# One new order for a whole backward pass: parameter gradients released early, and the dense branch put into the row order of the inverse transforms

## The chip, the cores and the metric

The kernel runs on one core of one Trainium2 chip. The core has five engines that work side by side: TensorE (PE in the profile, with its weight loads apart as PEld), VectorE (DVE), ScalarE (ACT), GpSimd (POOL) and SyncE (SP). Data moves between the chip's memory and the core's working memory by DMAs, which SP, ACT and POOL issue. The metric is the device time of one execution in microseconds (us). Before the change three executions took 793.69, 794.1 and 794.8 us, a median of 794.1.

## The reference

The forward pass mixes two branches with a gate that is worked out from each row of the input. The kernel returns the output and the gradients of fourteen of the inputs (15 results).

```python
def _A_ref(u, A_re, A_im, B_re, B_im, C_re, C_im, log_dt, Dskip):   # D = 448 channels, N = 256 states
    P = jnp.exp(logdA[:, :, None] * l[None, None, :])                # l = 0 .. 2047, rounded to bf16
    K = jnp.einsum("dn,dnl,dn->dl", Cc, P, dB).real
    ...                                                              # rfft of K and u, padded to 4096
    y = irfft(Uf * Kf)[:, :, 0, :L]
    y = y.transpose(0, 2, 1) + u * Dskip
    return y
def _B_ref(x, w1, b1, w2, b2):                                       # F = 1792
    h = relu(x @ w1 + b1) ** 2
    return h @ w2 + b2
g = sigmoid((x * gate_w).sum(-1, keepdims=True))                     # x is A_u, 2048 rows of 448
out = g * _A_ref(x, ...) + (1 - g) * _B_ref(x, ...)
# returned: out and the vjp of grad_out for A_u, the six A/B/C arrays, log_dt, Dskip, w1, b1, w2, b2, gate_w
```

## The kernel before, in words

The kernel is written in two steps. `build` records tasks: each is one instruction, one DMA, or a group of matmuls into one bank, with the tasks that it depends on. Two long lists in the file then fix everything. `ORDER` says in which order the tasks are emitted, and so the order of each engine's instructions; an entry is four times the task's number, plus a number that picks one of the engines or queues which the task allows (a copy can be ACT's or DVE's, a DMA SP's or POOL's). `HOMES` gives each buffer its place in one arena of working memory or in one of eight banks. An engine takes its instructions strictly in its part of the list, and SP and POOL take their DMAs so too. `R.dep` adds a dependency on a task that shares no data, so that a load does not start before a chosen moment.

All engine work is emitted from the helper's lines, which is why the profile knows only few lines: L1585 is every matmul, L1587 every transpose on PE, L1593 every activation, L1595 copies and DMAs, L1597 the other vector instructions, L1589 the transposing DMAs. Tiles of the arena all have the name "arena". Groups are told apart by their shapes.

The stages, in the order in which they begin:

- Forward transforms of the input `U` and of the gated gradient `DA` (`fwd1`, `fwd2`), their products, and a first inverse for the gradient of the convolution kernel K (lines 825 to 873). The spectra are stored to `sp_d`.
- Dense branch, forward (lines 1030 to 1051), in eight blocks of 256 rows. `turned` (line 1014) transposes a block on PE with the identity `ident` as the moving operand. `project` (line 975) writes the branch's result rows to a scratch tensor `br_d`.
- The gradient of w2 (lines 1053 to 1068): `DB2`, the whole of grad_out, is loaded in one DMA into a place that the dense branch has just left, and scaled by 1 - g on ACT and DVE (`omg32`). Then the dense branch's backward blocks (lines 1083 to 1105), which write a second `br_d` part and `dh_d`.
- Beside these, seven chunks c = 0 .. 6 of the state space. `tables(c)` (line 1159) builds powers X and Y and multiplies them into K's sums on PE; `gT[c]` is the last step of X. `gradient(c, h)` (line 1226) forms, for each half h, two products on DVE of 128x5376 and sums on PE, and stores 256 sums per row to `st_d`; `gG` holds its ends. `gG[11]` is chunk 5 done, `gG[13]` chunk 6.
- The gradient of w1 (lines 1270 to 1296): `U2`, the whole input, in one DMA; `dh_d` comes back through transposing DMAs on SP.
- The convolution kernel itself (lines 1298 to 1344): K's sums, `fwd1` and `fwd2` of K, eight products of 128x3584 with the stored spectra (`product`, two DVE instructions each; `gQ[0]` .. `gQ[7]`), and for each `inv1`, the first inverse stage, which stores to `hd[1]` (for the output) or `hd[2]` (for the gradient of the input). Each is read back whole, in another layout, by `load_hs`.
- The two last stages. Output (lines 1376 to 1394): for q = 0 .. 3 `load_hs`, `load_br`, the second inverse stage on PE, and per bank two instructions of DVE with 128x448 results (lines 1388 and 1389), 32 in all; their row sums give the gate's gradient. Gradient of the input (lines 1397 to 1415): the same loads from the other scratch tensors, PE, a copy, and the store. The rows of this stage lie in the order of the inverse transforms: partition 32 g + i holds what in the natural order is partition 4 i + g. So `load_br` uses four DMAs of 32 partitions.
- The gradient of gate_w (line 1416 on): the gate's gradient `ds_b` is first put back into natural rows with a matmul by `perm`, then multiplied with `U2`.
- Parameter gradients (line 1433 on; PR below), in two halves: chunks 0 to 3, with 128x512 operands, and chunks 4 to 6, with 128x384. Each half loads the sums `ST`, `pg` and `raw`, does 35 to 36 DVE instructions and two on ACT. Eight groups of transposes on PE, a sum for log_dt, and 24 stores follow. The loads of the first half depend on `gQ[0]`, those of the second on `gQ[6]`.

In the old list DVE has 834 instructions. The first half of PR has its places from 698 to 748, the second from 741 to 787, the last product of the spectra is at 737, and the output stage's instructions lie from 776 to 830, mixed with PR's last. On PE (779 tasks) the first inverse stages for `hd[1]` lie from 683 to 751, those for `hd[2]` from 716 to 747; PR's transposes are at 752 to 761, the output stage at 754 to 769. On SP the load of `ST0` is number 111.

Of the kernel before, what the change touches and what calls it, by code (L numbers as in the profile page):

```python
# [16 lines left out]
P = 128  # L17
L, D, N, F = 2048, 448, 256, 1792
LT = L // P
# [428 lines left out]
def replay(R, order, homes):  # L448
# [169 lines left out]
def build(nc, R, A_u, Ap, A_log_dt, A_Dskip, B_w1, B_b1, B_w2, B_b2, gate_w, grad_out, outs):  # L618
# [100 lines left out]
    s32, g32, omg32, omg2 = (R.buf(n, 32) for n in ("s32", "g32", "omg32", "omg2"))  # L719
    s_b, omg_b, gg = (R.buf(n, w) for n, w in (("s_b", 16), ("omg_b", 16), ("gg", 32)))  # L720
    g_b, gp_b = Sub(gg, 0), Sub(gg, 16)
    gt32, gpt_b = R.buf("gt32", 32), R.buf("gpt_b", 16)
    junk = R.buf("junk", 448)
    R.rank = 2.0
    for t in range(LT):
        V("scalar_tensor_tensor", out=junk.v(0, [[1, D]]), in0=U.v(D * t, [[1, D]]), scalar=1.0, in1=gwb.v(0, [[1, D]]), op0=MUL, op1=MUL, accum_out=s32.f(t, [[1, 1]]))
    al = [[1, LT]]
# [900 lines left out]
```

## Time and profile before

| what | value |
|---|---|
| median of the runs | 794.1 us |
| the profiled execution's own time | 792.28 us |
| span of its instructions | 790.5 us |
| PE busy | 649.5 us (82%) |
| DVE busy | 570.6 us (72%) |
| ACT busy | 472.8 us (60%) |
| POOL busy | 154.5 us (20%) |
| granted TensorE clock, mean | 0.929 |
| moved by DMA | 138.06 MB, mean 175 GB/s |

The busy time of PE counts modelled ends of pipelined matmuls, so a busy PE can still be short of its peak. "DMA share" is the mean busy share of the core's 16 DMA engines. Times in windows and rows count from the first instruction.

### The profile page before, as it was taken

How to read it: one execution, taken by the hardware profiler on the slowest of the kernel's cores; microseconds unless marked ns; L12 is line 12 of the kernel's file. 1: busy time of each engine (PE TensorE's matmuls, PEld its weight loads, DVE VectorE, ACT ScalarE, POOL GpSimd, SP SyncE). 2: the span in 40 equal slices, each digit the busy share in tenths (PEclk: the TensorE clock that was granted, in tenths of full speed). 3: DMA queues.
4: the chain of work that ended last, by engine and by line, in shares of the span. 5: the costliest groups of instructions: out<-in, count | busy, mean ns of one | idle time of the engine just before them, and what ended most of it. 6: DMA issues, size and time to landing. Idle time of an engine off the chain costs nothing.

```text
span 790.5 us, 24859 instructions
## 1 busy us (share of the span) xinstructions
PE 649.5 (82%) x11046; PEld 437.3 (55%) x11046; DVE 570.6 (72%) x866; ACT 472.8 (60%) x708; POOL 154.5 (20%) x262
## 2 busy tenths in 40 slices
PE   4678898969999789688887998798398889975577
PEld 4665466547676456365665766584366454652212
DVE  4698788759758878965984889379624168999882
ACT  4999988569779666546753464164234386645214
POOL 5312232210101111100111021001001101545342
PEclk9878999989999899999999999999799999999558
DMA  9637889652414455736552352416833654899995
GB/s 278 215 137 252 312 286 315 225 147 106 127 74 153 165 139 126 145 72 97 165 140 93 107 177 71 150 36 206 166 71 133 163 121 161 271 316 293 311 291 174
DMA packets 120366, 138.06 MB, mean 175 GB/s; under 512 B 75666, under 2 KB 103108, under 8 KB 119620
## 3 DMA queue, kind: packets, MB, share of 16 engines
q1 hardware_dynamic: 98148, 61.16, 29.5%
q0 software_dynamic: 18816, 73.63, 27.8%
q10 hardware_dynamic: 3296, 1.70, 0.8%
q8 instruction: 86, 1.41, 0.7%
q14 instruction: 20, 0.16, 0.1%
HBM read 60.01 MB, written 60.16 MB: 152 GB/s over the span
## 4 chain that ended last, share of the span: by engine, by line
PE 52%; DVE 18%; DMA 11%; ACT 10%; issue 7%; POOL 1%; ACTq 0%; SPq 0%; DVEq 0%; POOLq 0%
PE banks L1585 52%; DVE arena L1597 16%; ACT arena L1595 7%; DMA arena<-in_grad_out_dram 4%; DMA arena<-hd 3%; DVE arena L1595 2%; ACT arena L1593 2%; DMA hd<-arena 2%; DMA arena<-in_A_u_dram 1%; DMA arena<-br_d 1%; DMA arena<-in_B_w_dram 1%; ACT L1593 0%; POOL hd L1595 0%; POOL arena L1595 0%; ACTq L1595 0%
## 5 line engine op out<-in xcount | busy, mean ns | idle before, releaser
L1585 PE MATMUL banks<-arena 128*32 128x42 bf16 (+10 forms) x10998 | 643.9, 250 | 123.6 <-DVE arena L1597 39.6
L1585 PEld LDWEIGHTS <-arena 128*32 128x32 bf16 (+5 forms) x10994 | 432.4, 103 | 331.3 <-issue 180.2
L1597 DVE TENSOR_TENSOR arena<-arena 128x256 bf16<-128x256 bf16 (+13 forms) x502 | 385.7, 814 | 47.5 <-ACT arena L1593 25.1
L1595 ACT CAST arena<-banks 128x896 bf16<-128x896 f32 (+4 forms) x411 | 313.9, 827 | 165.3 <-PE banks L1585 138.9
L1595 DVE CAST arena<-banks 128x1024 bf16<-128x1024 f32 (+5 forms) x73 | 74.9, 1040 | 86.6 <-PE banks L1585 73.7
L1593 ACT ACTIVATE arena<-arena 128x256 f32<-128x256 f32 (+7 forms) x136 | 76.2, 583 | 48.9 <-DVE arena L1597 28.3
L1595 POOL DMA_DIRECT2D out_dram<-arena x60 | 32.5, 544 | 178.4 <-ACT arena L1595 98.9
L1597 DVE TENSOR_TENSOR arena<-banks,arena 128x1024 bf16<-128x1024 f32 (+2 forms) x46 | 40.5, 891 | 30.3 <-PE banks L1585 16.6
L1595 ACT COPY arena<-banks 128x168 f32<-128x168 f32 (+3 forms) x35 | 14.6, 427 | 60.7 <-PE banks L1585 49.7
L1597 DVE SCALAR_TENSOR_TENSOR arena<-arena 128x128 f32<-128x128 f32 (+1 forms) x86 | 30.2, 351 | 16.3 <-DMA arena<-in_A_u_dram 10.5
L1595 ACT COPY arena<-arena 128x256 bf16<-128x256 bf16 (+4 forms) x59 | 30.1, 553 | 14.3 <-DVE arena L1597 11.1
L1593 ACT ACTIVATE arena<-banks 128x1024 bf16<-128x1024 f32 (+1 forms) x29 | 26.0, 909 | 7.3 <-PE banks L1585 6.9
L1595 POOL DMA_DIRECT2D hd<-arena x36 | 23.0, 642 | 35.3 <-ACT arena L1595 30.6
L1595 POOL DMA_DIRECT2D br_d<-arena x21 | 11.7, 556 | 90.3 <-ACT arena L1595 90.1
L1595 ACT CAST arena<-arena 128x768 bf16<-128x768 f32 (+3 forms) x28 | 21.8, 789 | 9.9 <-DVE arena L1597 9.9
L1597 DVE SCALAR_TENSOR_TENSOR arena<-banks,arena 128x448 bf16<-128x448 f32 x32 | 19.8, 649 | 5.7 <-PE banks L1585 3.1
L1595 POOL DMA_DIRECT2D r_d<-arena x14 | 11.6, 825 | 61.7 <-ACT arena L1593 46.5
L1597 DVE TENSOR_SCALAR arena<-arena 128x448 bf16<-128x448 bf16 (+9 forms) x51 | 18.3, 394 | 6.9 <-PE banks L1585 5.1
L1595 POOL DMA_DIRECT2D dh_d<-arena x5 | 5.5, 1109 | 59.3 <-DVE arena L1597 44.4
L1587 PE MATMUL banks<-arena 128*128 128x128 bf16 (+1 forms) x48 | 5.8, 305 | 12.2 <-DVE arena L1597 12.2
L1595 POOL DMA_DIRECT2D st_d<-arena x8 | 4.4, 550 | 53.3 <-ACT arena L1595 53.3
L1595 POOL DMA_DIRECT2D arena<-in_grad_out_dram x19 | 11.7, 619 | 15.4 <-PE banks L1585 11.1
(46 smaller groups left out, 92.6 us busy)
## 6 DMA issues: line engine op xcount, KB each, us to landing
r_d<-arena POOLq DMA_DIRECT2D x14, 896.0 KB, 5.8
arena<-hd SPq DMA_DIRECT2D x12, 896.0 KB, 8.2
hd<-arena POOLq DMA_DIRECT2D x36, 224.0 KB, 6.4
sp<-arena POOLq DMA_DIRECT2D x7, 896.0 KB, 6.0
arena<-sp POOLq DMA_DIRECT2D x6, 896.0 KB, 8.7
dh_d<-arena POOLq DMA_DIRECT2D x5, 896.0 KB, 6.0
arena<-r_d SPq DMA_DIRECT2D x5, 896.0 KB, 6.1
out_dram<-arena POOLq DMA_DIRECT2D x28, 112.0 KB, 4.5
```

The lines of the kernel that those rows point to most:

```text
L1585: fn(out, **kw)
L1587: fn(out, kw["in_"], kw["ident"], **({"tile_position": kw["tile_position"]} if "tile_position" in kw else {}))
L1593: fn(out, kw.pop("in_"), kw.pop("func"), **kw)
L1595: fn(out, kw["in_"])
L1597: fn(out=out, **kw)
```

## The change

Five edits to the recording, and new lists for all of it:

1. PR's loads, both halves, depend on `gT[6]` (the last step of X for chunk 6) and, as before, on the sums that they read: the first half on chunks 0 to 3, the second on chunks 4 to 6 only for `ST1`.
2. The dense branch's rows take the order of the inverse transforms: `turned` multiplies by `perm` where it multiplied by `ident`, `DB2` and `U2` are loaded in four DMAs of 32 partitions each, and `DB2` is scaled by a turned `omgt32`, for which two small DVE instructions are added beside `gt32`.
3. `load_br` becomes one DMA of 128 partitions, eight times.
4. The matmul by `perm` and the copy ahead of the gradient of gate_w go away, with the second load of `perm`.
5. `ORDER` and `HOMES` are replaced as a whole: 2738 entries for 2757, 809 buffers for 810.

What the new list does around PR, read with the task numbers shifted by the added and removed tasks: DVE has 852 instructions. PR's first half lies from 669 to 717, among the last steps of chunk 6's tables (632 to 698) and ahead of the second product pair of chunk 5. Its second half lies from 757 to 796 (one scaling of `raw` earlier, at 674). The last product of the spectra is at 797 and 798, and the output stage follows from 799 to 848. On PE (778 tasks) chunk 6's gradient sums come at 641 and 666 (they were at 702 and 735), the first inverse stages for `hd[1]` from 681 to 723, those for `hd[2]` from 672 to 760, PR's transposes from 728 to 751, the sum for log_dt at 750, the output stage from 761 to 768. On SP the loads of `ST0`, `pg` and the second `pg` are numbers 83, 84 and 86, behind two quarters of `U2` and one transposing DMA, and ahead of seven more; on POOL both `raw` loads are numbers 162 and 163. Of the output stage's `load_hs`, one is ahead of the store of log_dt's row on SP (131) and three behind it (132, 133, 136). The last `load_hs` of the input's gradient has the place of the second half of `Gt`, which the output stage's last instructions read.

```diff
 ORDER = [
...
 HOMES = [
...
-    gt32, gpt_b = R.buf("gt32", 32), R.buf("gpt_b", 16)
+    gt32, gpt_b, omgt_b, omgt32 = R.buf("gt32", 32), R.buf("gpt_b", 16), R.buf("omgt_b", 16), R.buf("omgt32", 32)
...
+    V("tensor_scalar", out=omgt_b.v(0, al), in0=gt32.f(0, al), scalar1=-1.0, scalar2=1.0, op0=MUL, op1=ADD)
+    V("tensor_copy", out=omgt32.f(0, al), in_=omgt_b.v(0, al))
...
-        rh = ident.v(0, [[1, 128]])
+        rh = perm.v(0, [[1, 128]])
...
-    R.dma(DB2.v(0, [[1, LT * D]]), d(G2, 0, [[LT * D, P], [1, LT * D]]), ANY)
+    for g in range(4):
+        R.dma(DB2.v(0, [[1, LT * D]], 32 * g, 32), d(G2, g * LT * D, [[4 * LT * D, 32], [1, LT * D]]), ANY)
     for t in range(LT):
-        scaled(DB2.v(D * t, [[1, D]]), DB2.v(D * t, [[1, D]]), omg32.f(t, [[1, 1]]))
+        scaled(DB2.v(D * t, [[1, D]]), DB2.v(D * t, [[1, D]]), omgt32.f(t, [[1, 1]]))
...
-    R.dma(U2.v(0, [[450, 16], [1, D]]), d(u2, 0, [[LT * D, P], [D, 16], [1, D]]), ANY)
+    for g in range(4):
+        R.dma(U2.v(0, [[450, 16], [1, D]], 32 * g, 32), d(u2, g * LT * D, [[4 * LT * D, 32], [D, 16], [1, D]]), ANY)
...
-    perm = const("perm", q=("POOL",), rank=300.0)
...
-        for g in range(4):
-            R.dma(br.v(0, [[2 * D, 2], [1, 2 * D]], 32 * g, 32), d(br_d, w * P * LT * D + g * LT * D + 2 * q * D, [[4 * LT * D, 32], [8 * D, 2], [1, 2 * D]],
-                  [("br", w, 2 * q + x + 8 * hp) for x in range(2) for hp in range(2)]), ANY if g % 2 else ("POOL", "SP"))
+        R.dma(br.v(0, [[2 * D, 2], [1, 2 * D]]), d(br_d, w * P * LT * D + 2 * q * D, [[LT * D, P], [8 * D, 2], [1, 2 * D]], [("br", w, 2 * q + x + 8 * hp) for x in range(2) for hp in range(2)]), ANY)
...
-    ps = R.ps("dsn")
-    dsn = R.buf("dsn", 16)
-    R.group("PE")
-    mm(ps.f(0, al), perm.v(128, [[1, 128]]), ds_b.v(0, al), True, True)
-    R.end(also=[dsn])
-    V("tensor_copy", out=dsn.v(0, al), in_=ps.f(0, al))
...
-        mm(ps.f(0, [[1, D]], 0, 1), dsn.v(t, [[1, 1]]), U2.v(450 * t, [[1, D]]), t == 0, t == LT - 1)
+        mm(ps.f(0, [[1, D]], 0, 1), ds_b.v(t, [[1, 1]]), U2.v(450 * t, [[1, D]]), t == 0, t == LT - 1)
...
-        R.dep = (gQ[0 if c0 == 0 else 6],)
+        R.dep = (gT[6],)
```

298 rows, old and new, of tables (HOMES, ORDER) are left out of this document.

## The prediction

> **What bounds the kernel now.** I began with the busy slices of the page.
>
> ```profile
> span 790.5 us, 24859 instructions
> DVE  4698788759758878965984889379624168999882
> DMA  9637889652414455736552352416833654899995
> ```
>
> Each digit is 19.8 us. PE is the busiest engine over the span, but what it does up to about 560 us is nearly kept by the new list, as the windows below will show. From slice 33 (652 us) on, DVE and DMA are both near full, while DVE is nearly idle in slices 29 to 32. The windows say how much, and how far the lists agree.
>
> ```profile
> 0.00:560.00 560.00, 467.01 (x8181) 333.26 (x8181) 425.80 (x675) 365.90 (x559) 92.57 (x153) 0.95 0.54 162
> 540.00:560.00 20.00, 9.84 (x133) 4.66 (x115) 19.69 (x27) 5.78 (x10) 3.21 (x6) 0.79 0.67 177
> 560.00:660.00 100.00, 84.76 (x1893) 56.55 (x1894) 40.78 (x33) 50.99 (x65) 6.45 (x12) 0.94 0.49 115
> 560.00:720.00 160.00, 138.41 (x2590) 89.58 (x2591) 96.92 (x80) 85.96 (x115) 32.86 (x56) 0.96 0.65 180
> 660.00:780.00 120.00, 92.46 (x937) 45.70 (x935) 104.02 (x160) 53.55 (x82) 53.36 (x93) 0.83 0.92 291
> 720.00:740.00 20.00, 5.77 (x52) 3.23 (x51) 19.03 (x36) 6.28 (x9) 9.38 (x17) 0.72 0.90 283
> ```
>
> After the length come PE, PEld, DVE, ACT and POOL, each with its instructions, then PE's clock, the DMA share and GB/s. Up to 560 PE works 467 us; added up in the order of each list, each group by its old duration, 468 us of PE work stand ahead of the last table sums of chunk 6 in the old list and in the new. I give that part no gain and no loss, with 3 us either way for reshuffled waits. From 560 to 660 DVE works 41 us of 100 and DMA half the time; from 660 to 780 DVE works 104 of 120 and DMA 92%. In 720 to 740 PE is idle for 14 of 20 us. The last third is a DVE and DMA queue, with PE waiting. The timeline shows the hand-over:
>
> ```profile
> 721.36 3.01 PE L1585 MATMUL banks<-arena 64*128 64x448 bf16 x30 [1.80 <-DVE arena L1597]
> 723.12 8.11 DVE L1597 TENSOR_TENSOR arena<-arena 128x512 f32<-128x512 f32 x14
> 731.67 10.04 DVE L1597 TENSOR_TENSOR arena<-arena 128x384 f32<-128x384 bf16 x20 [0.45 <-ACT arena L1593]
> 735.12 1.98 SPq L1595 DMA_DIRECT2D arena<-hd  x3
> 739.63 2.66 PE L1585 MATMUL banks<-arena 64*32 64x448 bf16 x18 [0.68 <-DMA arena<-hd]
> 741.64 1.26 DVE L1597 SCALAR_TENSOR_TENSOR arena<-banks,arena 128x448 bf16<-128x448 f32 x2
> 772.29 0.62 DVE L1597 SCALAR_TENSOR_TENSOR arena<-banks,arena 128x448 bf16<-128x448 f32 x1
> ```
>
> The last first-stage inverse runs from 721.4; it belongs to the output, so all of `hd[1]` is late, and its reads are issued only at 735. Meanwhile DVE does PR until about 748 (the two rows alone are 18 us). The output stage's 32 DVE instructions run from 741.6 to 772.9, 31.3 us, and 17.6 us pass from there to the end. The chain of waits has these pieces in it:
>
> ```profile
> 260.53 9.34 DMA arena<-in_grad_out_dram
> 688.39 11.17 DMA arena<-in_grad_out_dram
> 739.88 9.47 DMA arena<-hd
> 772.12 7.13 DMA arena<-br_d
> ```
>
> The last three are loads in a crowded DMA system, the last of all a quarter of `br`; the first is `DB2`.
>
> **PR's size.** DVE's groups by shape, from 674 us to the end:
>
> ```profile
> L1597 DVE SCALAR_TENSOR_TENSOR arena<-banks,arena 128x448 bf16<-128x448 f32 x32 | 19.8, 649 | 5.7 <-PE banks L1585 3.1 <-DMA out_dram<-arena 2.5
> L1597 DVE TENSOR_TENSOR arena<-arena 128x512 f32<-128x512 f32 x19 | 12.8, 684 | 0.1
> L1597 DVE TENSOR_TENSOR arena<-arena 128x384 f32<-128x384 f32 x19 | 10.2, 553 | 0.3
> L1597 DVE TENSOR_TENSOR arena<-arena 128x256 bf16<-128x256 f32 x10 | 5.9, 612 | 0.1
> L1597 DVE TENSOR_TENSOR arena<-arena 128x192 bf16<-128x192 f32 x10 | 4.7, 489 | 0.1
> L1597 DVE TENSOR_TENSOR arena<-arena 128x512 f32<-128x512 bf16 x6 | 4.0, 681 | 0.0
> L1597 DVE TENSOR_TENSOR arena<-arena 128x384 f32<-128x384 bf16 x6 | 3.3, 554 | 0.6 <-ACT arena L1593 0.4
> L1597 DVE TENSOR_SCALAR arena<-arena 128x512 bf16<-128x512 bf16 x1 | 0.4, 422 | 0.0
> L1595 DVE CAST arena<-arena 128x4 bf16<-128x4 f32 x4 | 0.7, 166 | 0.1
> L1597 DVE TENSOR_SCALAR arena<-arena 128x128 bf16<-128x128 bf16 x3 | 0.8, 251 | 0.6 <-ACT arena L1595 0.6
> L1595 DVE CAST arena<-banks 128x896 bf16<-128x896 f32 x2 | 2.2, 1092 | 2.0 <-PE banks L1585 2.0
> ```
>
> The first half is 12.8 + 5.9 + 4.0 = 22.7, with its scaling 23.1 us; the second 10.2 + 4.7 + 3.3 = 18.2, with its scaling 18.5. Of these 41.6 us, 23 lie behind the last product of the spectra now.
>
> **The change part by part.**
>
> *PR's first half.* Its 23.1 us move from 675-727 to behind the last table steps of chunk 6, some 555 to 595. Cover: the 59 us that DVE idles in 560 to 660. Without it they delay chunk 6's table sums, which wait in DVE's queue behind the first of these instructions, and with them K's sums on PE.
>
> *PR's second half.* Its 18.5 us now come before the last two product pairs, beside PE's w1 gradient. In all, 23 us more of DVE work stand ahead of the last product. The hole holds them, if the sums of chunk 6 come early; the new list has them 61 to 69 places earlier on PE.
>
> *PE.* PR's transposes and the sum for log_dt move ahead of the last inverse stage:
>
> ```profile
> L1587 PE MATMUL banks<-arena 128*128 128x128 bf16 (+1 forms) x48 | 5.8, 305 | 12.2 <-DVE arena L1597 12.2
> 749.40 4.45 PE L1585 MATMUL banks<-arena 64*32 64x448 bf16 x13 [1.92 <-DMA arena<-hd]
> ```
>
> The sum is the last 3.3 of the second row's 4.45 (two fp32 passes, 750.2 to 753.6). Together 9.1 us. PE idles 160 - 138.4 = 21.6 us in 560 to 720, so this may cost from 0 to 9 us.
>
> *The last product's time.* Bounds: 718, if the idle time of DVE and PE takes all; 730, if PE pays its 9.1 in full (721.4 + 9.1). I take 722.5, nearer to the first, since the holes of DVE (59) and PE (21.6) are larger than what goes in (23 and 9.1).
>
> *From there to the end.* Now 790.5 - 721.4 = 69.1 us. After the change PR is gone from it, and `hd[1]` is complete long before. Hand-over: two `load_hs` of 896 KB stand on SP behind the store of log_dt's row, which waits for PR's last instruction, the sum and a copy; that is about when the last product ends. So a load, then PE:
>
> ```profile
> arena<-hd SPq DMA_DIRECT2D x8, 896.0 KB, 7.7
> arena<-br_d SPq DMA_DIRECT2D x19, 112.0 KB, 4.3
> arena<-pg_d POOLq DMA_DIRECT2D x1, 1024.0 KB, 6.0
> ```
>
> 7.7 + 2.8 for the issue and PE's first group (739.6 to 741.6 now) = 10.5; at least 7, if the loads are earlier and only the last inverse stage (4 us) and PE stand before. The output pass: 32 x 0.649 = 20.8, and 5 for the rest of it in the new list (twelve of about 0.17, four scalings of 0.25, a copy of 1.1, and under 1 of seams) = 26, against 31.3 now. The end: 17.6 now, of which 7.1 is the last `br` load; in its place comes the last `load_hs` (7.7), which waits for the pass's end because its place is `Gt`'s. So 18. Sum 10.5 + 26 + 18 = 54.5, or 14.6 less than now.
>
> *DMAs.* Four loads become one, eight times: 24 issues fewer. A quarter lands in 4.3 us, 896 KB in 7.7; one of 448 KB lies between, and they are issued ahead, so I put 0 on it (bounds -3 and +3). `DB2` and `U2` become four issues each. The `DB2` load is 9.3 us on the chain, at 260.5, but the w2 gradient that needs it stands in both lists behind chunk 1's sums on PE; 0, bounds -2 and +2. The Trainium skill, "DMA: Bandwidth & Descriptors", Rules for kernel authors, says that transfers to disjoint partition parts share the same DMA engines, and that one of 128 partitions should be used. By that rule the split loads win nothing and the joined one saves only issues, so the sum would be the same; no row here compares the two forms.
>
> *Small edits.* Two DVE instructions of about 0.17 us at the gate, beside PE's transforms; a matmul of 0.2 and a copy of 0.17 fewer at the end, off the chain; one small load on POOL fewer. 0.
>
> **The sum.** 722.5 + 54.5 = 777.0 of span, against 790.5. The profiled execution takes 1.8 more than its span (792.28), and the median of the runs is 1.8 above that: 777.0 + 3.6 = **780.6**.
>
> A check by bytes: 660 to 780 moves 0.291 MB/us x 120 = 34.9 MB. Both `pg`, both `raw` and `ST0` leave it, 1024 + 768 + 640 + 480 + 1024 KB = 4.0 MB, for a time with half the DMA share free. 30.9 / 0.291 = 106 us, so 13.8 less, if DMA is what limits: nearly the same answer by another way.
>
> **The rivals.**
>
> *PE pays.* Chunk 6's sums and PR's transposes crowd PE, whose busy time there was 138 of 160 us. Last product 730.5, span 785, time 788.6. For: PE has no gap for 45 us now, where it does this work,
>
> ```profile
> 651.37 45.23 PE L1585 MATMUL banks<-arena 128*128 128x128 bf16 x566 [0.15 <-ACT arena L1595]
> ```
>
> and against it are the idle 21.6 us.
>
> *Better.* Last product at 718, and the output stage's loads not behind the store: 718 + 7 + 26 + 18 = 769, time 772.6. For: both holes; against: every handover would have to fit.
>
> *The queue blocks (slower).* DVE works strictly in order. PR's first instruction stands among chunk 6's table steps and needs `ST0` and `pg`, which start only after the last step of X (about a third of the way into the first row below, 543), on SP behind a transposing DMA:
>
> ```profile
> 535.02 25.76 DVE L1597 TENSOR_TENSOR arena<-arena 128x256 bf16<-128x256 bf16 x38
> 551.66 4.61 SPq L1589 DMA_TRANSPOSE arena<-dh_d  x2
> 560.83 1.75 PE L1585 MATMUL banks<-arena 128*32 128x128 bf16 x96 [9.20 <-DVE arena L1597]
> ```
>
> If they start at 552 and take 6 to 11 us in a system at 0.67, they land at 558 to 563, where DVE wants them at about 555: 3 to 8 us, which the hole absorbs. But PR's 23 us behind them also stand ahead of chunk 5's and 6's remaining products, and PE has only chunk 5's and 6's sums and the w1 gradient to do. If PE has no cover, the whole 23.1 are lost: 777 + 23.1 = 800.1, time 803.7. It decides once more than 13.5 us of it reach the last product. For: PE's strict order and its 9.2 us of waiting for DVE at 560. Against: w1's gradient stands there in both lists. The Trainium skill ("TensorE: Matmul & The Clock Gate", Architectural detail) says the same of the queue, that VectorE is strictly first in, first out; the trace's DVE order agrees in all 834 instructions, and the rule alone gives this rival no other price.
>
> *No gain.* The loads moved early push the transposing DMAs and `U2` back, and the DMA system is as late at the end as now: 792 to 796.
>
> **Chances.** The forecast 0.42 (own range 776 to 786), PE pays 0.19, better 0.15, no gain 0.08, the queue blocks 0.16. The range 768 to 794 leaves out about 0.2: nearly all of the slow case, part of no gain, and a little of the better one. A difference under 0.2%, 1.6 us, can't be told from none. Faster: 0.42 + 0.19 + 0.15, and 0.01 of no gain: 0.77. Same 0.07, slower 0.16.
>
> **What would show it.** PR's 128x512 instructions at 550 to 600 instead of 675 to 727; DVE above 60 us in 560 to 660; no PR instruction between the last 128x3584 and the 128x448 ones; the output pass in some 26 us; DMA share above 0.55 in 560 to 660. PE waiting more than 15 us for DVE or for `ST0` between 550 and 600 would show the blocked queue. A last product later than 730, or an output pass that waits for `hd`, would make the forecast wrong.

## The result, and the profile after

| kernel | median | lowest to highest | runs |
|---|---|---|---|
| before, timed again beside it | 793.69 us | 788.61 to 801.45 | 15 |
| after | 789.38 us | 787.45 to 792.25 | 15 |

The ratio is 0.9941, with a 95% interval of 0.9917 to 0.9966: faster by 0.6%, 4.3 us, where 13.5 us were forecast. The changed kernel ran in two more groups: 789.82 us (0.9956, 0.9926 to 0.9986) and 788.27 us (0.9910, 0.9876 to 0.9944). In the tables below, medians are over all runs of a kernel, while ratios leave out runs that the chip disturbed; so the two can differ by a little.

In the changed file the helper's lines lie five lower: L1580 is every matmul, L1590 copies and DMAs, L1592 the other vector instructions. First the page's busy slices, then the windows, with the same columns as before.

```profile
span 790.5 us, 24806 instructions
...
DVE  4579768758678967984888589659897336879683
...
DMA  8916888645332465663392535527890444789897
```

```profile
0.00:560.00 560.00, 464.98 (x8181) 328.31 (x8181) 425.06 (x684) 360.07 (x546) 100.82 (x168) 0.95 0.57 163
540.00:560.00 20.00, 10.60 (x217) 7.33 (x214) 19.55 (x38) 7.84 (x14) 4.47 (x7) 0.81 1.08 275
560.00:660.00 100.00, 72.94 (x1796) 49.66 (x1797) 58.89 (x62) 34.30 (x48) 4.33 (x8) 0.82 0.51 117
660.00:780.00 120.00, 106.77 (x1038) 54.31 (x1036) 95.87 (x139) 67.87 (x93) 42.38 (x74) 0.89 0.85 273
720.00:740.00 20.00, 18.05 (x151) 10.76 (x148) 19.37 (x31) 12.41 (x18) 9.61 (x17) 1.00 0.97 308
```

DVE has gained 18.1 us of work in 560 to 660 (58.89 against 40.78) and lost 8.2 in 660 to 780. PE, idle for 14 of 20 us in 720 to 740 before, is busy for 18. So the end was relieved as meant. But PE did 72.94 us of work in 560 to 660 where it did 84.76: the middle fell behind.

Two marks split the span: the end of the last step of X for chunk 6, and the end of the last product of the spectra. The later is the end of the fourth row below (732.21 + 10.16 = 742.4). "Tail" is the span less that end, here and below from unrounded times.

| profile | X of chunk 6 ends | chunk 5's last product ends | last product of the spectra ends | span | tail |
|---|---|---|---|---|---|
| before | 543.1 | 599.0 | 721.3 | 790.5 | 69.2 |
| after | 552.0 | 616.6 | 742.4 | 790.5 | 48.1 |
| after, second profile | 550.0 | 614.1 | 740.0 | 787.0 | 47.0 |
| after, third profile | 551.7 | 616.4 | 742.9 | 790.4 | 47.6 |

The tail became 21.6 us shorter in the mean of the three, and the last product 20.4 us later. In the traces alone the two nearly cancel (mean span 789.3 against 790.5). That the times differ by 4.3 is because the profiled execution of before (792.28) lies 1.4 below its median, and the one of after (792.25) is the slowest of its 15.

The timeline of after, at four places: the early transforms, the table steps of chunk 6, the last product with the hand-over to the output pass, and that pass.

```profile
35.85 2.42 PE L1580 MATMUL banks<-arena 112*128 112x112 bf16 x24 [8.00 <-DMA arena<-in_A_B_im_dram]
...
565.29 7.67 DVE L1592 TENSOR_TENSOR arena<-arena 128x512 f32<-128x512 f32 x5 [3.75 <-DMA arena<-pg_d]
...
573.01 3.75 PE L1580 MATMUL banks<-arena 128*32 128x128 bf16 x229 [19.99 <-DVE arena L1592]
...
732.21 10.16 DVE L1592 TENSOR_TENSOR arena<-arena 128x3584 bf16<-128x3584 bf16 x10
...
749.03 2.40 DVE L1592 SCALAR_TENSOR_TENSOR arena<-banks,arena 128x448 bf16<-128x448 f32 x4 [6.67 <-ACT arena L1590]
...
757.64 3.52 PE L1580 MATMUL banks<-arena 128*128 128x448 bf16 x20 [4.57 <-DMA arena<-br_d]
```

Two waits are new: 8.0 us of PE for a small load at 36 us, and 3.75 us of DVE for `pg` at 565. A third has grown: PE waits 20.0 us for DVE behind it, where it was 9.2. So chunk 6's table sums on PE start at 573.0 instead of 560.8: of these 12.2 us, 8.9 are the later end of X, and 3.3 come between X and the sums. At the end, the output pass follows the last product in 6.7 us.

The chain of waits in the tail now ends in work, with less of it waiting for loads:

```profile
744.48 7.18 DMA out_dram<-arena
...
751.67 5.93 DMA arena<-br_d
...
766.09 15.05 PE banks L1580 x86
```

Of DMAs the chain has one store (7.2 us) and one `br` load (5.9 us) in the tail, and then 15 us of PE's own matmuls; the loads of `hd` that stood there are gone. This chain is followed back only to 729 us. In the third profile it reaches further, and there it has no load of `grad_out` behind 545 us, but it has the load of `pg`, issued behind a transposing DMA on SP:

```profile
553.47 11.81 DMA arena<-pg_d
```

### The profile page after: what moved, and what is told of

It is laid out like the page before. It is cut to its first block, busy times and chain, and to the rows that moved or that the text cites. A ratio compares the mean times of both kernels' runs of the same rounds, so it can differ in the third digit from the quotient of the medians.

```text
span 790.5 us, 24806 instructions
## 1 busy us (share of the span) xinstructions
PE 648.5 (82%) x11045; PEld 433.3 (55%) x11045; DVE 581.9 (74%) x884; ACT 464.7 (59%) x691; POOL 151.2 (19%) x256
## 5 line engine op out<-in xcount | busy, mean ns | idle before, releaser
L1580 PE MATMUL banks<-arena 128*128 128x128 bf16 (+11 forms) x10997 | 645.4, 250 | 134.2 <-DVE arena L1592 42.2
L1580 PEld LDWEIGHTS <-arena 128*128 128x128 bf16 (+7 forms) x10993 | 430.3, 104 | 344.2 <-issue 167.7
L1592 DVE TENSOR_TENSOR arena<-arena 128x128 f32<-128x128 f32 (+14 forms) x501 | 386.7, 812 | 69.8 <-ACT arena L1590 27.7
L1590 ACT CAST arena<-banks 128x896 bf16<-128x896 f32 (+5 forms) x407 | 310.9, 829 | 168.9 <-PE banks L1580 144.0
L1590 DVE CAST arena<-banks 128x1024 bf16<-128x1024 f32 (+4 forms) x76 | 79.4, 1054 | 72.9 <-PE banks L1580 55.7
L1588 ACT ACTIVATE arena<-arena 128x256 f32<-128x256 f32 (+9 forms) x135 | 77.6, 594 | 47.9 <-DVE arena L1592 18.2
L1592 DVE TENSOR_TENSOR arena<-banks,arena 128x1024 bf16<-128x1024 f32 (+2 forms) x46 | 40.5, 890 | 21.8 <-PE banks L1580 12.7
L1590 POOL DMA_DIRECT2D out_dram<-arena x55 | 29.9, 546 | 109.9 <-ACT arena L1590 86.6
L1590 ACT COPY arena<-banks 128x168 f32<-128x168 f32 (+3 forms) x35 | 14.5, 427 | 60.4 <-PE banks L1580 59.1
L1592 DVE SCALAR_TENSOR_TENSOR arena<-arena 128x128 f32<-128x128 f32 (+1 forms) x86 | 30.1, 350 | 12.1 <-DMA arena<-in_A_u_dram 10.4
L1590 ACT COPY arena<-arena 128x256 bf16<-128x256 bf16 (+4 forms) x52 | 28.1, 592 | 15.4 <-DVE arena L1592 15.1
L1590 ACT CAST arena<-arena 128x768 bf16<-128x768 f32 (+3 forms) x27 | 21.4, 798 | 19.2 <-DVE arena L1592 19.2
L1590 POOL DMA_DIRECT2D br_d<-arena x22 | 12.2, 554 | 78.7 <-ACT arena L1590 69.5
L1590 POOL DMA_DIRECT2D r_d<-arena x16 | 13.3, 835 | 67.0 <-ACT arena L1588 47.7
L1590 POOL DMA_DIRECT2D st_d<-arena x11 | 6.1, 552 | 104.2 <-ACT arena L1590 104.2
L1592 DVE SCALAR_TENSOR_TENSOR arena<-banks,arena 128x448 bf16<-128x448 f32 x32 | 18.9, 648 | 9.3 <-ACT arena L1590 6.7
L1590 POOL DMA_DIRECT2D hd<-arena x31 | 19.6, 635 | 31.5 <-ACT arena L1590 30.5
L1588 ACT ACTIVATE arena<-banks 128x1024 bf16<-128x1024 f32 (+1 forms) x25 | 22.6, 923 | 3.6 <-PE banks L1580 3.5
L1592 DVE TENSOR_SCALAR arena<-arena 128x448 bf16<-128x448 bf16 (+10 forms) x54 | 18.4, 381 | 3.2 <-DMA arena<-in_grad_out_dram 2.9
L1590 POOL DMA_DIRECT2D dh_d<-arena x6 | 6.7, 1110 | 66.3 <-DVE arena L1592 60.6
L1590 DVE CAST arena<-arena 128x384 bf16<-128x384 f32 (+8 forms) x28 | 12.8, 455 | 2.1 <-ACT arena L1588 1.7
L1590 POOL DMA_DIRECT2D arena<-in_grad_out_dram x19 | 11.7, 618 | 11.7 <-PE banks L1580 11.5
```

Of the source, the lines that this page charges most:

```text
L1580: fn(out, **kw)
L1588: fn(out, kw.pop("in_"), kw.pop("func"), **kw)
L1590: fn(out, kw["in_"])
L1592: fn(out=out, **kw)
```

## The experiments

All edits are to the changed kernel, except in three that edit the kernel before (named so). In the diffs an entry of `ORDER` is four times a task's number plus the pick of its engine; only the entries of the engine in question are shown.

### PR's first half behind chunk 5's last product

The first edit leaves PR's loads where the change put them, but moves the first half's 36 DVE instructions, its two on ACT and one scaling behind the last product of chunk 5. The second also issues the waiting `dh_d` transposes first on SP.

```diff
-10464, ... 10624, ... 10460, 10468, ... 10576, ... 10608, ... 8180,
+8180, 10464, 10624, 10460, 10468, ... 10576, 10608,
```

> The changed kernel with one thing moved: the vector instructions of PR's first half (and the one scaling of raw for the second) stand behind the last gradient product of chunk 5 instead of among the last table steps of chunk 6; their loads stay where they are. Theory A, the block in DVE's strict queue costs time: DVE no longer waits for pg and ST0 at 561 to 565, the sums of chunk 6 on PE start at about 568 instead of 574.7, chunk 5's last product ends at about 595 instead of 616.6, and the kernel takes 781 to 785 us, against 789.4. Rival B, PE has nothing else to do there in any case and the 23 us come back in front of K's transform: 788 to 791. Rival C, it is the loads and not the instructions that cost: no change either, with the transposing DMAs as late as before (575 to 590).

> As the run with PR's first half moved behind, and beside it three transposing DMAs of the w1 gradient stand on SP ahead of the loads of ST0 and pg instead of behind them. Rival C, the crowded DMA system: the w1 sums on PE start by about 575 instead of 598, and this run is 4 to 8 us faster than the one without the second move. Theory A: no more than 2 us between the two.

Measured: 797.99 us (1.0058, 1.0017 to 1.0099) and 797.75 us (1.0031, 0.9990 to 1.0072). Both are some 8 us slower than the changed kernel; none of the three theories had that (781 to 791 us). The timeline of the first:

```profile
565.09 3.78 PE L1580 MATMUL banks<-arena 128*32 128x128 bf16 x229 [15.79 <-DVE arena L1592]
...
737.80 9.91 DVE L1592 TENSOR_TENSOR arena<-arena 128x3584 bf16<-128x3584 bf16 x10
```

PE's wait for DVE shrinks from 20.0 to 15.8 us, and the sums start 8 us earlier (565.1 against 573.0); yet the last product ends at 747.7, 5.3 us later: the queue was freed as theory A had it, and the time was lost again behind chunk 5. So the change's place for PR is the better of the two: its 23 us lie more under cover among chunk 6's table steps than behind them. Most of PE's wait is not PR's either, since 15.8 us of it stay. And the order of the transposes, moved on top of this, changes nothing that can be measured.

### The wait for `pg` alone

PR's first instruction, the only one of its half that stood so early, is moved behind the last table step of chunk 6.

```diff
-10464, ... 7980, 7984, 8008, 7988, 10624, 8000,
+7980, 7984, 8008, 7988, 10624, 8000, 10464,
```

> The changed kernel with one vector instruction moved: the first of PR, which waits 4.0 us for pg at 561 to 565, stands behind chunk 6's last table steps instead of ahead of four of them. Theory H, DVE's queue sets the end of this stage: the table sums of chunk 6 start on PE 4 to 5 us earlier behind the last step of X (18 to 19 us instead of 23), and 3 to 5 us of it reach the end: 785 to 787. Rival: PR's later instructions and PE's later work swallow it, 788.5 to 790.5.

Measured: 787.10 us (0.9914, 0.9878 to 0.9950), 2 to 2.7 us below the changed kernel.

```profile
567.84 3.79 PE L1580 MATMUL banks<-arena 128*32 128x128 bf16 x229 [15.73 <-DVE arena L1592]
569.44 4.74 DVE L1592 TENSOR_TENSOR arena<-arena 128x512 f32<-128x512 f32 x7
...
728.42 9.92 DVE L1592 TENSOR_TENSOR arena<-arena 128x3584 bf16<-128x3584 bf16 x10
```

DVE no longer waits for `pg`, PE waits 4.3 us less, and the last product ends at 738.3, 4.1 us earlier than in the first profile of after; counted from the end of X it is 3.3. The blocked queue is real in the traces. Its price of 2 to 4 us is less sure: the intervals of the two ratios overlap, and the changed kernel did not run beside this one.

### How much of PR's first half is hidden

20 of its 36 DVE instructions work on an eighth of their width; the gradients of A, B, C and log_dt for chunks 0 to 3 are left out by it. The first run cuts the changed kernel, the second the kernel before.

```diff
+if c0 == 0 and o.buf.name in full:
+    o, a, b = cut(o), cut(a), cut(b)      # last dimension / 8
+full.add(o.buf.name)
```

> The changed kernel with 20 of the first half's 36 vector instructions cut to an eighth of their width (the gradients of A, B, C and log_dt of chunks 0 to 3 are not computed); some 0.5 to 0.55 us less for each, 10 to 11 us less DVE work at 575 to 605. Theory I, about half of PR's first half is hidden at its new place: 4 to 6 us faster, 784 to 786. If all is hidden, no change (789 to 790); if none, 779.

> The kernel before the change with the same 20 instructions cut to an eighth of their width (the same gradients are not computed). There they stand between 674 and 727, where DVE works without a pause. If all of it lies on the path that sets the end, as the forecast took it: 9 to 11 us faster, 783 to 785 where the kernel before takes 794; if the loads and the spectra's products set that stage, 0 to 4 us.

Measured: 788.29 us (0.9949, 0.9910 to 0.9987) and 794.97 us (0.9979, 0.9936 to 1.0023). DVE's busy time falls by 10 us in the changed kernel (581.9 to 571.7) and by 9 in the kernel before (570.6 to 561.7). In the changed kernel that gains about 1 us, which is within the noise: what was cut of PR is hidden there, as forecast. In the kernel before it gains nothing that can be measured, though DVE was near full around it. Two more runs of the kernel before asked why: one loads only 16 of 128 partitions of `ST0`, `pg` and `raw` (2.4 MB less; the same gradients are left out), the other does both cuts.

```diff
+NP = 16 if c0 == 0 else P
-..., d(st_d, ..., [[NCK * 512, P], ...
+..., 0, NP), d(st_d, ..., [[NCK * 512, NP], ...
```

> The kernel before the change with the three loads of PR's first half (ST0, pg, raw) cut to 16 of 128 partitions, 2.35 MB less between 660 and 680 (the gradients of A, B, C and log_dt of chunks 0 to 3 are not computed from the right data); the vector instructions keep their full width. Theory J, the tail of the kernel before is set by the DMA system and by DVE about equally: alone this wins 0 to 3 us (791 to 794). Theory K, the DMA system alone sets it: 2.35 MB at 0.291 MB/us are 8 us, so 785 to 788. Theory L, neither, only the order of hd does: 793 to 795.

> The kernel before the change with both cut: the loads of PR's first half to 16 partitions and 20 of its 36 vector instructions to an eighth of their width (the same gradients are not computed). Theory J: only both together free the stage, 784 to 788. Theory K: as with the loads alone, 785 to 788. Theory L: 793 to 795.

Measured: 793.85 us (0.9975, 0.9947 to 1.0003) and 794.87 us (1.0006, 0.9975 to 1.0036). No gain that can be measured from either or from both; by the last interval, both together are worth 2 us at most. DVE's waits and the windows from 660 to 726, before and then with both cuts:

```profile
DVE arena L1597 <- DMA arena<-sp: 1.3, 2, 0.8
...
660.00:726.00 66.00, 56.66 (x728) 34.62 (x726) 62.11 (x57) 38.77 (x55) 29.87 (x50) 1.00 0.93 290
```

```profile
DVE arena L1606 <- DMA arena<-sp: 10.1, 4, 4.5
...
660.00:726.00 66.00, 57.15 (x722) 34.48 (x722) 53.22 (x57) 37.04 (x53) 27.93 (x48) 0.97 0.86 249
```

(The second row of each: length, then PE, PEld, DVE.) DVE's work falls by 8.9 us, and its waits for the stored spectra grow by 8.8. It was full for 62 of 66 us, and not the bound: the spectra's loads came just behind it. POOL issues them at 683.1, 702.4 and 706.2 us with the cuts and at 683.0, 702.9 and 707.3 without, in its list behind stores of `hd`; the cuts did not bring them forward. What sets their time beyond that was not tested.

### The hole on PE filled with the gradient of w1

PE's wait among chunk 6's sums is offered w1's sums: transposes first on SP, `pg`'s instruction behind, and of the four sums of w1's first block of columns two ahead of chunk 6's table sums and two among them.

```diff
-8204, ... 8448, ... 8496, ... 8452, ... 8500, ...
+8448, 8452, 8456, 8460, 8464, 8496, 8500, 8504, 8508, 8512, 8204,
```

> The changed kernel with PE's hole at 553 to 573 and 580 to 598 filled: three transposing DMAs of the w1 gradient ahead of ST0 and pg on SP, the four sums of the first quarter of the w1 gradient (some 4 us each) on PE ahead of and between the turns and the table sums of chunk 6 instead of from 598 on, and PR's first instruction on DVE behind chunk 6's last table steps, so that nothing waits for pg. Theory F: PE is the bound from 553 to about 700 and what is idle there is lost; 8 to 14 us of PE's idle time are won, the last product ends at 728 to 734 instead of 742, and the time is 776 to 783. Rival G: from 600 on it is DVE's chain (chunk 6's products, copies, spectra, PR's second half) that sets the last product, whatever PE has left to do; then no more than 3 us are won, 786 to 790.

Measured: 795.27 us (1.0004, 0.9972 to 1.0036), 6 us slower than the changed kernel; both theories had it faster. PE's longest wait from 550 to 600:

```profile
PE banks L1580 <- DMA arena<-dh_d: 14.0, 1, 14.0
```

PE does more work in this stretch, 25.0 us of 50 against 18.0. But the hole only shrank, from 20.0 to 14.0 us; now it waits for the transposed `dh_d`, chunk 6's sums queue behind, and chunk 5's last product ends at 622.9 instead of 616.6. Before 566 us PE has nothing of w1 that is ready; the theory that the cover was only badly ordered fell.

### The early loads

The last step of X ends 8 us later in after though PE does no more work up to 560 us, and the first wait of the timeline has just that size. `B_im`, 224 KB, is issued on SP at 8.35 and used at 35.85; in before it stood on POOL, at 4.85. DMA issues from 0 to 45 us (name, queue, count, KB each, us from issue to landing) and the queues' packets and MB, before, then after:

```profile
q0 software_dynamic: 1821, 7.82, 49.6%
q1 hardware_dynamic: 2512, 2.56, 21.0%
...
arena<-in_A_B_im_dram POOLq DMA_DIRECT2D x1, 224.0 KB, 13.1
arena<-in_A_C_re_dram SPq DMA_DIRECT2D x1, 224.0 KB, 14.1
```

```profile
q0 software_dynamic: 1712, 7.36, 51.1%
q1 hardware_dynamic: 2096, 2.29, 19.3%
...
arena<-in_A_C_re_dram SPq DMA_DIRECT2D x1, 224.0 KB, 25.9
arena<-in_A_C_im_dram POOLq DMA_DIRECT2D x1, 224.0 KB, 14.4
```

The same 224 KB takes 14 us on POOL and 26 on SP in after, and 14 on SP in before. Large loads lie beside them on POOL. A 1 MB load of constants is issued at 15.4 in before and at 10.7 in after; two of w1, of 1344 and 1568 KB, at 21.4 and 35.0 in before and at 18.8 and 20.2 in after. The first of them:

```profile
15.39 0.53 POOL L1595 DMA_DIRECT2D arena<-c_M  x1
```

```profile
10.68 0.56 POOL L1590 DMA_DIRECT2D arena<-c_M  x1 [3.07 <-DMA arena<-in_A_u_dram]
```

The repair puts `B_im` on POOL next to `B_re`, three small constants ahead of the 1 MB one, and a 1344 KB part of w1 one place back. It is tried alone, and on top of the w1 edit. (60 is `B_im` on SP, 61 on POOL; 76 is the 1 MB load.)

```diff
-56, ... 76, ... 80, ... 84, ... 88, 60,
+56, 61, ... 80, 88, 84, 76,
```

> The changed kernel with the order of some loads in the first 35 us as it was before the change: B_im is loaded on POOL's queue behind B_re instead of on SP, MI, perm and NMI stand ahead of the 1 MB of M2, and the 1344 KB of w1 behind its 224 KB part. Theory D: most of the 9 us by which the table steps of chunks 1 to 6 end later than before the change come from PE's single wait of 8.0 us for B_im near 36 us; then that wait is under 2 us, X of chunk 6 ends at about 545 instead of 552, and the kernel takes 781 to 786. Rival E: that wait is covered later, or the lag is the new order of the stages; then 788 to 790 with X of chunk 6 at about 551.

> The run with the w1 sums as cover, and beside it the early loads in the order of the kernel before (B_im behind B_re, 1 MB of M2 and 1344 KB of w1 later). If both causes add, this is 2 to 4 us faster than the run with the cover alone; 773 to 781 by theory F, 784 to 788 by rival G.

Measured: alone 786.98 us (4 runs; 0.9891, 0.9829 to 0.9954), 2.4 us less than after, a difference that four runs cannot tell from none; on the w1 edit 791.87 us (0.9916, 0.9869 to 0.9962), 3.4 less than without it. PE's waits in the first 60 us of the repaired kernel:

```profile
PE banks L1580 <- DMA arena<-in_A_u_dram: 10.0, 1, 10.0
...
PE banks L1580 <- DMA arena<-in_B_b_dram: 1.9, 1, 1.9
```

Before and after wait 10.5 and 10.4 us for the same first load; the 8 us for `B_im` are gone, and 1.9 of them came back. X of chunk 6 ends at 548.8 and 545.3 in the two, and at 547.1 and 546.2 in two more with this repair (below), against 551.2 in the mean of after. Single profiles spread, though: in those of other edits that leave the early loads as in after it is 547.8 to 552.9, so only the means tell. The old list has 543.1 in before, and 539.6 and 540.5 in two profiles with cuts. So the repair gives back 4.4 of 8 to 10 us, about half of the lateness; the rest comes of the other rearrangements ahead of X and was not taken apart. Nor was it taken apart which of the repair's moves counts most, `B_im`'s to POOL or the large loads'.

### The joined load of `br`

`load_br` is four DMAs of 32 partitions again, on two chips.

```diff
-        R.dma(br.v(0, [[2 * D, 2], [1, 2 * D]]), d(br_d, w * P * LT * D + 2 * q * D, [[LT * D, P], ...
+        for g in range(4):
+            R.dma(br.v(0, [[2 * D, 2], [1, 2 * D]], 32 * g, 32), d(br_d, w * P * LT * D + 32 * g * LT * D + 2 * q * D, [[LT * D, 32], ...
```

> The changed kernel with each load of br again as four transfers of 32 partitions, two on POOL and two on SP, at the place of the one. The forecast put 0 on the joining, with -3 to +3 as bounds: 788 to 791 by it. Rival: the 24 more issues stand in the full queues of the last 50 us and each takes its turn; then 792 to 795, and the end behind the last product is 51 us or more, against 48.1.

> The changed kernel with each br load again as four transfers of 32 partitions, once more and beside the changed kernel itself: the first comparison (793.4 against 789.4 and 789.8 on other chips) left 4 us that its trace did not show. If the joining is worth 3 us or more it takes 792.5 to 794 here against 789.5; if not, within 1.5 us of the changed kernel.

> The changed kernel itself once more, as the measure for the runs beside it and for what one profiled execution can be off: 787 to 792 us. If the lag of the table steps behind those of the kernel before is a property of the list, X of chunk 6 ends again at 548 to 552 and PE again waits some 8 us for B_im near 36 us; if it was a chance of one execution, it ends near 543.

> The changed kernel itself as the measure for the three runs beside it on the same chip: 788 to 791 us, as the two times before.

Measured: 793.42 us (1.0002, 0.9961 to 1.0043) and 793.71 us (0.9986, 0.9953 to 1.0018): neither differs from the kernel before. The changed kernel beside them has 789.82 and 788.27. With the runs pooled that the ratios use, 22 with four loads have a median of 793.71, 32 with one load 789.05: about 4 us. The issues from 660 us on, after, then with four (the second run):

```profile
arena<-br_d POOLq DMA_DIRECT2D x6, 448.0 KB, 6.7
arena<-br_d SPq DMA_DIRECT2D x2, 448.0 KB, 5.9
```

```profile
arena<-br_d SPq DMA_DIRECT2D x16, 112.0 KB, 6.6
arena<-br_d POOLq DMA_DIRECT2D x16, 112.0 KB, 6.0
```

A load of 448 KB lands as soon after its issue as one of 112 KB. Four in a row cost more than one: the first four behind the last product took 10.3 us from the first issue to the last landing (748.2 to 758.5, first run), the one load in their place 5.9. The Trainium skill, "DMA: Bandwidth & Descriptors", Rules for kernel authors, says of two transfers to disjoint partition halves that they share the same engines, and to use one of 128 partitions instead; for quarters, the times here agree. The output pass takes 27.6 and 27.8 us with four loads against 24.2, 3.5 us more, but the stretches on both sides of it are shorter, so that only 1.6 us of the gain show in the whole tail (49.1 and 49.3 us against 47.0 to 48.1); where the rest lies stays open.

### The order of the last two products

The product for the output and the one for the input's gradient trade places in every queue, with their buffers, and the reads of `hd` for the output stand behind the stores of the last product, as in the kernel before.

```diff
-9573, 9576, 9580, ... 9813, 9816, 9820, ...
+9813, 9816, 9820, ... 9573, 9576, 9580, ...
```

> The changed kernel with the last pair of spectra exchanged: the product of rank 411, which belongs to the output, and the one of rank 415, which belongs to the gradient of the input, take each other's places in all queues and buffers (load, two vector instructions, four groups on PE, copies, stores), and the reads of hd for the output stand behind the stores of the last product, as in the kernel before. The same work, bytes and instructions. Theory L, the tail of the changed kernel is short because hd for the output is complete before the last product: the output stage on PE starts some 10 to 14 us later behind the last product, and the time is 798 to 803 instead of 789. If the work and the loads of PR moved out of the tail are what made it short: 789 to 792.

Measured: 805.25 us (4 runs; 1.0139, 1.0072 to 1.0205), 16 us slower than the changed kernel, with the same work. Its timeline:

```profile
746.09 3.69 PE L1580 MATMUL banks<-arena 64*128 64x448 bf16 x34 [0.50 <-ACT arena L1590]
...
756.54 1.33 SPq L1590 DMA_DIRECT2D arena<-hd  x3
...
763.29 6.12 PE L1580 MATMUL banks<-arena 64*32 64x448 bf16 x38 [13.51 <-DMA arena<-hd]
```

The last product ends at 743.9, 1.5 us later than in after; then the old hand-over is back: store `hd`, read it, and PE waits 13.5 us, with a tail of 61.3 us against 47 to 48. PR isn't in that tail.

### The repairs together

The early loads, `pg`'s instruction behind, and, in the tail, two groups of w1's last sums on PE ahead of log_dt's sum, so that a store and a `br` load come earlier.

```diff
-10780, ... 8820, ... 8824,
+8820, 8824, 10780,
```

> Three repairs together on the changed kernel: the early loads in the order of the kernel before (B_im behind B_re, M2 and the 1344 KB of w1 later), PR's first instruction behind chunk 6's last table steps, and in the tail two w1 sums on PE with their copy and their store ahead of the sum for log_dt, so that the br load of the second group, whose place that store leaves free, is issued at about 743 instead of 748.6. If each is worth what its wait measures in part: 3 + 4 + 3, so 779 to 782. If they are covered, 785 to 788.

> The version with the three repairs (early loads, PR's first instruction behind the table steps, the br load of the second group released earlier) once more: 783 to 786, against 788 to 790 for the changed kernel.

Measured, on two chips: 784.59 us (6 runs; 0.9866, 0.9820 to 0.9911) and 781.51 us (6 runs; 0.9852, 0.9807 to 0.9897): faster than both kernels, by some 1.4% against before. Of the second, the length and two rows:

```profile
span 781.2 us, 24808 instructions
```

```profile
562.89 3.72 PE L1580 MATMUL banks<-arena 128*32 128x128 bf16 x228 [15.69 <-DVE arena L1592]
...
722.62 9.91 DVE L1592 TENSOR_TENSOR arena<-arena 128x3584 bf16<-128x3584 bf16 x10
```

The last product ends at 732.5, 9.8 us earlier than in after, and the tail is 48.7: all of the gain is ahead of the last product. With the edit in the tail, the second group of the output stage starts on PE 12.0 us behind the last product instead of 15.3, but the end comes no sooner. The two groups of runs of this one kernel differ by 3 us, so differences of 2 us between groups of runs are not to be trusted alone.

Not tried: PR's first half early in the old list, PR spread over DVE's later holes in the new one, and the old tail without PR's second half.

## Why the prediction was right and wrong

The direction was right, and the time lies in the range. The size was not: on the traces the last product came 19 us later than forecast, and the tail was 7 us shorter. That the time lies in the range, and within 1 us of the 788.6 of the rival "PE pays", is luck: two errors of opposite sign nearly cancel.

| term | forecast | after (mean of three) | off |
|---|---|---|---|
| up to X of chunk 6 | no change | 551.2 against 543.1 | +8.1 |
| from there to the last product of the spectra | 178.2 + 1.1 | 190.5 | +11.2 |
| last product to the end | 54.5 | 47.6 | -6.9 |
| span | 777.0 | 789.3 | +12.3 |

(178.2 = 721.3 - 543.1; 1.1 = 722.5 - 721.4; the terms add up but for a rounding of 0.1.)

1. **"Up to 560 no gain and no loss": the step that failed first.** It compared PE work ahead of a point, 468 us in both lists. The work was nearly equal indeed (467.01 and 464.98 us in the window), but not the waits: a load that had landed 13.1 us after its issue on POOL stood on SP beside large loads that now came earlier, and PE lost 8 us at 36 us. The bound of 3 us for reshuffled waits had no row behind it. About half of the 8.1 is shown by the repair; the rest is open.
2. **The middle.** The forecast let DVE's 59 idle us and PE's 21.6 take the 23 + 9.1 us of moved work, for 1.1 us. Against before it took 12.3 us more, of which 8.6 fall between X and chunk 5's last product (55.9 to 64.5 us). The wait for `pg` is part of it: the rival **"the queue blocks"** named instruction, load and waiting engine rightly, with DVE's wait at 3.75 us (3 to 8 forecast) and PE's above 15. The size came partly by luck: `pg` landed at 565.3, later than the 558 to 563 named, and DVE wanted it at 561.5, later than 555. The rival's other half, all 23 us of PR lost, was wrong: of 10 us cut there only 1 came back, and a place with less cover costs 8 us more. So the forecast's cover held for the part of PR that was cut. From X to the last product the run without the wait for `pg` is 3.3 us shorter than after and still 9.0 longer than before; the cause of these 9.0 us stays open.
3. **"PE pays"** had the last product at 730.5; it came at 741.8. What PE did there was wait (20 us for DVE), not work: 128.95 us busy in 560 to 720 against 138.41.

```profile
560.00:720.00 160.00, 128.95 (x2466) 82.69 (x2468) 109.70 (x101) 78.87 (x104) 20.89 (x36) 0.86 0.60 160
```

4. **The tail** was right in kind and better in size. Hand-over 6.7 us (10.5 forecast, at least 7), output pass from 749.0 to 773.2, 24.2 us (26), the end 17.3 us (18). The prediction named two causes, PR gone and `hd[1]` complete early. The stages of the tail tell them apart (hand-over: from the last product to the first 128x448 instruction; pass: to the end of the 32nd; means of the profiles):

| profiles | hand-over | output pass | end | tail |
|---|---|---|---|---|
| before | 20.3 | 31.3 | 17.6 | 69.2 |
| before, PR's first half cut, loads and work | 19.8 | 31.4 | 18.1 | 69.4 |
| after (three) | 6.8 | 24.2 | 16.6 | 47.6 |
| after, last two products exchanged | 20.5 | 22.3 | 18.6 | 61.3 |
| after, four `br` loads (two) | 5.7 | 27.7 | 15.8 | 49.2 |

The hand-over is `hd`'s: with the products exchanged it takes 20.5 us without any PR in it, as long as the 20.3 before, where DVE did PR in all of it. So PR's 20 us there were under cover, and `hd[1]` complete early is worth 13 to 14 us of tail and 16 us of time. The cuts in the kernel before can't show that: they took some 3 us of PR's work out of the hand-over and left the second half. Of the 7.1 us that the output pass became shorter, the joined `br` loads are about 3.5; the rest may be PR's instructions that are gone from it, which no run shows alone. The hand-over was sized from `load_hs` behind log_dt's store, but the first `load_hs` was issued ahead of that store, at 734.8, and had landed at 740.8.
5. **The joined `br` loads, put at 0 (-3 to +3):** about 4 us, just beyond the bound. That is nearly the whole gain of 4.3: without it the new lists gain nothing that can be measured.
6. **The check by bytes** counted 4.0 MB as gone from 660 to 780. 0.273 x 120 = 32.8 MB moved there, 2.1 less than before. It agreed with the sum only because both took the last third as the whole story.

Of the signs named beforehand, these came: PR's 128x512 instructions at 565 to 606, none of PR between the last 128x3584 and the 128x448 ones, a short output pass. DVE in 560 to 660 came to 58.9, just under 60. The DMA share there is 0.51, not above 0.55: the moved loads were issued from 552.8 to 555, behind `U2`'s quarters, and the share rose in 540 to 560, from 0.67 to 1.08. The last product at 742 is later than 730, which was named as what would make the forecast wrong.

## What to carry to other kernels

When a whole order is replaced, compare when each early load is needed and what large load now stands beside it, not only the work ahead of a point: equal work had 8 us of lateness here. A tail is set by whose data are complete last; ask which of two equal branches has the longer hand-over, and finish that one first (16 us here). And a near-full engine is not a bound until less work on it has been shown to shorten the run: 9 us less on DVE, at 62 of 66 us busy, gave nothing.

## What the runs showed of the hardware

Not expected was how far a small load on SP falls behind large ones on POOL: 25.9 us against 14.4 for the same 224 KB, in one kernel and one window. In these 45 us POOL's queue moved 7.36 MB in 1712 packets, SP's 2.29 MB in 2096, so 4.3 KB each against 1.1 KB. From 10 to 20 us, with loads waiting in both, the counts are nearly equal: 534 packets and 2.22 MB on POOL, 525 and 0.35 MB on SP. The Trainium skill, "DMA: Bandwidth & Descriptors", Queues, rings and completion order, says that each DMA engine takes turns between its queues packet by packet. That fits these ten microseconds; from 20 to 30 us the counts are 483 and 873, which it does not explain by itself. No run here changed the packets' size alone. Also new was that a load of 448 KB and one of 112 KB took the same 6 to 7 us to land at the same places of the changed list; in the kernel before, the quarters on SP took 4.3.
